# Sigmoid attention with a squared-ReLU MLP on one core: attn @ v in quarters of the array, and all eight PSUM banks as four tiles in turn

## The chip, the core and the metric

The kernel runs on one core of a Trainium2 chip. The core has a matrix engine (TensorE, in the profile PE, with its weight loads as PEld), a vector engine (DVE), a scalar engine (ACT), GpSimd (POOL), and a sync engine (SP) that issues the DMAs here. Each engine works through its own queue in order; semaphores make an engine wait for another. Matmul results land in PSUM, which this kernel uses as eight banks of 512 fp32 numbers on each of 128 partitions. The metric is the device time of one launch in microseconds. The kernel before takes 1073.21 us, the median of 3 runs (1072.75 to 1073.55).

## What is computed

```
def _attn_ref(q, k, v):                       # (8, 12, 448, 64) each
    scores = q @ k.T / sqrt(64) - log(448)
    return sigmoid(scores) @ v

def _moe_ref(x, w_in, w_out):                 # x: 3584 x 768, the heads side by side
    r = maximum(x @ w_in, 0)                  # 768 x 2048
    return (r * r) @ w_out                    # 2048 x 768
```

## The kernel before

There are two stages. The first is the attention, in 24 **blocks** of two **pairs**; a pair is two heads of one batch entry. `pairs` counts 48 pairs, and block d works on pairs n = 2d and n + 1. Beside the attention, this stage also converts the MLP's weights. The second stage is the MLP: `gemm1` and `gemm2`, each with seven products in place of eight on 2 x 2 blocks. The change only touches the first stage and the way in which PSUM is handed out.

For one pair, the transposed q and k of both heads lie in one tile `x` (head j on partitions 64j to 64j + 63). `high` (L489) and `low` (L493), both on DVE, split it into two parts of lower precision, `qh` and `ql`. The 448 keys are three tiles of 128 (NT = 3) and a rest of 64 (KR = 64).

- `scores` (L276): for each key tile, three passes (high with high, low with high, high with low) of two matmuls, one per head, each with 64 rows of weights by 128 columns. The form is written 64*128 in the profile, and the two run side by side in the array. The result, 128 keys by 2 heads x 448 queries, is a PSUM tile `sc` of two banks; ACT turns it into `at` by one sigmoid (L259).
- `scores_rest` (L292): the 64 left-over keys of both pairs in one PSUM tile `sr`, four matmuls in the form 64*64, one for each quarter of the array.
- `attn_v_rest` (L304): the left-over keys times v, four matmuls 64*64. They start the sums of both pairs, which are the two banks of one PSUM tile (`pav` in the profile).
- `attn_v` (L313): the three key tiles times v, two matmuls 128*64 side by side for each, added to the same sums.
- `put_x`: the sums go to SBUF as `xo`; ACT copies those of the first pair (L320), DVE those of the second (L322). From batch entry 2 on, SP stores them to HBM.

Each fp32 matmul of `scores_rest`, `attn_v_rest` and `attn_v` stands in the trace as two of equal shape.

The weights arrive as 64-bit words. `convert_words` (L147, L148, on ACT) and `convert_join` (L152, L153, L156 on DVE, then L159 on POOL) turn half a chunk into numbers, and `sums` (L168 to L171, DVE) forms four sums per chunk. A chunk is three pieces, numbered k; `weights_of` deals 40 pieces out over 43 places, one place for each pair.

The order on each engine is written by hand in `block(d)` under `manual_schedule`: what stands earlier in `block` is earlier in each queue. At the head of block d stand ACT's copy of pair n - 2, the weight piece of place n - 2, `high(n + 3)`, DVE's copy of pair n - 1, and `low(n + 3)`. Then come the scores of pairs n and n + 1, the left-over scores of the *next* block, `attn_v_rest`, another `high` and `low` around the weight piece of place n - 1, the ACT words, and `attn_v`.

In the attention, PSUM is three two-bank tiles `sc` in rotation and one two-bank tile `duo`. The two sums `pav` live in `duo`, and one of the six score tiles of each block (the first of the second pair; another one in the last block) also uses it.

Of the kernel before, what the change touches and what calls it, by code (L numbers as in the profile page):

```python
# [19 lines left out]
P = 128  # L20
# [50 lines left out]
def sigmoid_attention_relu2_mlp(  # L71
# [189 lines left out]

    def score_tile(name):
        return ps.tile([P, 2, 512], F32, tag="sc", bufs=3, name=name)[:, :, :S]

    def scores(b, p, x, passes=((0, 0), (1, 0), (0, 1))):

        out = []

        other = (0, 2) if (b, p) >= (B - 1, NP - 2) else (1, 0)
        for t in range(NT):  # L270
            sc = (duo if (p % 2, t) == other else score_tile)(f"sc_{b}_{p}_{t}")
            ks = slice(t * P, (t + 1) * P)
            for n, (kp, qp) in enumerate(passes):
                for j in range(2):
                    rows = slice(j * D, (j + 1) * D)
                    nc.tensor.matmul(  # L276
                        sc[:, j],
                        x[kp][rows, 1, ks],
                        x[qp][rows, 0],
                        start=(n == 0),  # L280
                        stop=(n == len(passes) - 1),
                    )
            out.append(sigmoid(f"at_{b}_{p}_{t}", sc))
        return out

    def scores_rest(d, xs):

        sc = score_tile(f"sr_{d}")
        for r, x in enumerate(xs):
# [6 lines left out]

    def attn_v_rest(d, rest, vt):

        sums = duo(f"pav_{d}")
        pavs = [sums[:, r] for r in range(2)]  # L300
        for r in range(2):
            for j in range(2):
                rows, columns = slice(r * KR, (r + 1) * KR), slice(j * D, (j + 1) * D)
                nc.tensor.matmul(  # L304
                    pavs[r][columns], vt[rows, 2 * NT, columns], rest[rows, j], start=True, stop=False
                )
        return pavs

    def attn_v(n, pav, at, vt):
        for t in range(NT):  # L310
            for j in range(2):
                columns = slice(j * D, (j + 1) * D)
                nc.tensor.matmul(  # L313
                    pav[columns], vt[:, n % 2 * NT + t, columns], at[t][:, j], start=False, stop=(t == NT - 1)
                )

    def put_x(b, p, pav, scalar=False):
        x = op1(f"xo_{b}_{p}")
        if scalar:
            nc.scalar.copy(out=x, in_=pav)  # L320
        else:
            nc.vector.tensor_copy(out=x, in_=pav)  # L322
        if b < KEPT:
# [75 lines left out]
    todo = [(m, i) for m in range(2) for i in range(NI) if m == 0 or i not in DEFERRED]  # L399
    x, vt, xs, at, pav, f64, w, rest = {}, {}, {}, {}, {}, {}, {}, {}  # L400
    ready, stores, later = [], [], []
# [30 lines left out]
    def block(d):  # L432

        n = 2 * d
        more = n + 2 <= last
        for m in (n + 5, n + 6):
            load(m)
# [5 lines left out]
        if d == 0:  # L445
            for m in (1, 2, 3):
                high(m)
                low(m)
            score(0, (x[0],), ((0, 0),))
            rest[0] = scores_rest(0, (x[0], x[1]))  # L450
# [46 lines left out]

    def put(n, scalar=False):
        stores.append(put_x(*pairs[n], pav.pop(n), scalar))

# [22 lines left out]

    def duo(name):
        return ps1.tile([P, 2, 512], F32, tag="duo", bufs=1, name=name)[:, :, :S]

    def bank(name):
        return ps2.tile([P, 512], F32, tag="bank", bufs=6, name=name)[:, :S]

# [216 lines left out]
    with tc.manual_schedule():  # L746
        with tc.tile_pool(name="ps", bufs=3, space=PSUM) as ps:
            wp = ps.tile([P, 2, 512], F32, tag="sc", bufs=3, name="warm_ps")[:, :, :S]
            for i in range(8):
# [6 lines left out]
            for k in range(2):  # L756
                weights_load(k)
            load(4)
            for d in range(len(pairs) // 2 - 2):
# [14 lines left out]
        ps2 = ctx.enter_context(tc.tile_pool(name="ps2", bufs=6, space=PSUM))  # L774
        work = [
# [64 lines left out]
```

## Time and profile before

| quantity | before |
|---|---|
| median of 3 runs | 1073.21 us |
| the profiled execution, its own time | 1072.65 us |
| its span, first to last instruction | 1070.9 us |
| attention, 4.2 to 249.8 us of the span: length | 245.6 us |
| busy in it: PE / DVE / ACT / POOL | 245.4 / 196.1 / 201.6 / 60.9 us |
| granted TensorE clock | 1.000 |

A row of the timeline has the start in us from the span's start, the length in us, the engine, the line of the kernel, the operation, output <- input with the shapes, a count where several are merged, and in brackets the idle time before it with what ended it. A row of groups has the same names, then busy time and the mean length of one in ns, then idle time before it. A matmul's length includes its way through the array, so neighbours overlap: the pace of the array is read from the distance between starts, not from lengths.

### The profile page before, as it was taken

The page shows a single profiled execution, that of the slowest core. Times are in us where ns is not written, and L with a number is a line of the kernel's source. Part 1 is how long each engine was busy: PE and PEld are TensorE (multiplying, and loading weights), DVE is VectorE, ACT ScalarE, POOL GpSimd, SP SyncE. Part 2 cuts the span into 40 slices and gives each one's busy share as a digit, 9 for nine tenths or more (in the row PEclk, how much of TensorE's full clock was granted, in tenths as well). Part 3 has the DMA queues.
Part 4 walks back from the last instruction along what each step waited for, and adds up shares of the span by engine and source line. Part 5 has one row for each costly group of instructions (what it writes and reads, how often), then busy time and mean ns, then how long its engine had stood idle before and what let it go on. Part 6 is the DMA issues. An engine that isn't in the chain of part 4 may idle for free.

```text
span 1070.9 us, 14914 instructions
## 1 busy us (share of the span) xinstructions
PE 1066.0 (100%) x5858; PEld 888.4 (83%) x5858; DVE 765.5 (71%) x865; ACT 621.1 (58%) x772; POOL 75.5 (7%) x42
## 2 busy tenths in 40 slices
PE   9999999999999999999999999999999999999998
PEld 4555555557999999999999999999999999999997
DVE  6887888776688898645579884456897925579941
ACT  7887888876767765433455653344565523455721
POOL 1222232210111000000000000000000000000000
PEclk9999999999999999999999999999999999999999
DMA  9989999882576445533343465333335633333441
GB/s 360 391 291 323 376 378 335 323 284 66 183 257 212 128 144 188 183 112 104 103 140 97 145 210 183 104 103 104 115 118 195 204 105 120 120 97 109 144 144 52
DMA packets 83446, 196.80 MB, mean 184 GB/s; under 512 B 6704, under 2 KB 57776, under 8 KB 83376
## 3 DMA queue, kind: packets, MB, share of 16 engines
q1 hardware_dynamic: 83376, 195.85, 53.1%
q8 instruction: 46, 0.75, 0.3%
q14 instruction: 24, 0.20, 0.0%
HBM read 154.53 MB, written 41.29 MB: 183 GB/s over the span
## 4 chain that ended last, share of the span: by engine, by line
PE 98%; DVE 1%; ACT 0%; issue 0%; ACTq 0%; DVEq 0%
PE ha L534 22%; PE oa L534 22%; PE hb L534 11%; PE ob L534 11%; PE pav L313 10%; PE sc L276 8%; PE hc L534 5%; PE oc L534 5%; PE sr L292 2%; PE pav L304 2%; PE warm_ps L750 0%; DVE xo L358 0%; ACT w_1h L236 0%; DVE xo L322 0%; ACT xt_0h L329 0%
## 5 line engine op out<-in xcount | busy, mean ns | idle before, releaser
L237 DVE TENSOR_TENSOR w_1l<-w_1l,w_1h 128x1536 fp32r<-128x1536 f32 x60 | 105.9, 1766 | 72.7 <-ACT w_1h L236 72.1
L577 ACT COPY s<-ha 128x448 f32<-128x448 f32 x96 | 51.0, 531 | 132.7 <-PE ha L534 122.9
L259 ACT ACTIVATE at<-sc 128x896 f32<-128x896 f32 x144 | 119.3, 934 | 10.5 <-PE sc L276 10.5
L313 PE MATMUL pav<-at,v 128*64 128x448 f32 x576 | 113.5, 543 | 0.0
L236 ACT CAST w_1h<-w_1l 128x1536 fp32r<-128x1536 f32 x60 | 88.8, 1480 | 19.6 <-DMA w_1l<-w 19.6
L313 PEld LDWEIGHTS pav<-at,v 128*64 128x64 f32 x576 | 39.2, 137 | 72.7 <-issue 72.2
L237 DVE TENSOR_TENSOR w_5l<-w_5l,w_5h 128x1152 fp32r<-128x1152 f32 x32 | 43.3, 1354 | 45.3 <-ACT w_5h L236 45.3
L159 POOL TENSOR_TENSOR a<-a,f 128x768 int32<-128x768 int32 x26 | 60.9, 2343 | 160.0 <-ACT at L259 64.4
L236 ACT CAST w_0h<-w_0l 128x1536 fp32r<-128x1536 f32 x28 | 41.5, 1480 | 47.8 <-DMA w_0l<-w 47.8
L237 DVE TENSOR_TENSOR w_0l<-w_0l,w_0h 128x1536 fp32r<-128x1536 f32 x28 | 49.2, 1756 | 18.9 <-ACT w_0h L236 18.6
L276 PE MATMUL sc<-qh 64*128 64x448 f32 x282 | 54.2, 381 | 0.2 <-DVE xo L322 0.2
L493 DVE TENSOR_TENSOR ql<-x,qh 128x896 fp32r<-128x896 f32 x47 | 54.1, 1151 | 0.1
L236 ACT CAST w_5h<-w_5l 128x1152 fp32r<-128x1152 f32 x32 | 37.1, 1158 | 25.5 <-DMA w_5l<-w 25.3
L276 PE MATMUL sc<-qh,ql 64*128 64x448 f32 x282 | 51.5, 362 | 0.0
L276 PE MATMUL sc<-ql,qh 64*128 64x448 f32 x282 | 51.4, 361 | 0.0
L614 DVE TENSOR_TENSOR g<-hb,s 128x448 f32<-128x448 f32 x32 | 19.9, 622 | 42.5 <-PE hb L534 42.5
L560 DVE SCALAR_TENSOR_TENSOR g<-g 128x896 f32<-128x896 f32 x40 | 43.6, 1090 | 1.1
L276 PEld LDWEIGHTS sc<-qh 64*128 64x128 f32 x282 | 26.4, 184 | 19.2 <-issue 12.7
L489 DVE CAST qh<-x 128x896 fp32r<-128x896 f32 x47 | 32.5, 691 | 8.6 <-DMA x<-qk 8.6
L702 ACT COPY t<-oa 128x448 f32<-128x448 f32 x36 | 19.1, 530 | 33.6 <-PE oa L534 33.2
L608 ACT ACTIVATE g<-ha 128x448 f32<-128x448 f32 x32 | 17.4, 544 | 31.7 <-PE ha L534 31.7
L534 PE MATMUL oa<-o_0h,w_0h 128*128 128x448 f32 x96 | 35.1, 365 | 0.0
(522 smaller groups left out, 3070.8 us busy)
## 6 DMA issues: line engine op xcount, KB each, us to landing
w_1l<-w SPq DMA_DIRECT2D x60, 768.0 KB, 4.5
w_0l<-w SPq DMA_DIRECT2D x28, 768.0 KB, 4.5
x<-qk SPq DMA_DIRECT2D x47, 448.0 KB, 7.0
f<-w_in SPq DMA_DIRECT2D x16, 768.0 KB, 8.0
w_5l<-w SPq DMA_DIRECT2D x32, 384.0 KB, 4.0
v<-v SPq DMA_DIRECT2D x24, 448.0 KB, 7.6
outT<-o SPq DMA_DIRECT2D x47, 224.0 KB, 2.4
w<-s SPq DMA_DIRECT2D x13, 768.0 KB, 9.6
```

Source lines behind the costliest of these rows:

```text
L159: nc.gpsimd.tensor_tensor(out=wb, in0=wb, in1=t.bitcast(I32)[:, :, 0], op=ALU.add)
L236: nc.scalar.copy(out=hi, in_=raw)
L237: nc.vector.tensor_sub(out=lo, in0=raw, in1=hi.bitcast(F32))
L259: nc.scalar.activation(at, sc, AF.Sigmoid, bias=NEG_LOG_S, scale=SCALE)
L276: nc.tensor.matmul(sc[:, j], x[kp][rows, 1, ks], x[qp][rows, 0], start=(n == 0), stop=(n == len(passes) - 1),)
L292: nc.tensor.matmul(sc[r * KR : (r + 1) * KR, j], x[rows, 1, NT * P :], x[rows, 0], start=True, stop=True)
L313: nc.tensor.matmul(pav[columns], vt[:, n % 2 * NT + t, columns], at[t][:, j], start=False, stop=(t == NT - 1))
L489: nc.vector.tensor_copy(out=xs[n][0], in_=x[n])
L493: nc.vector.tensor_sub(out=xs[n][1], in0=x[n], in1=xs[n][0].bitcast(F32))
L534: nc.tensor.matmul(out, a[:, c], b, start=first and n == 0, stop=last and n == 2, skip_group_check=True)
L560: nc.vector.scalar_tensor_tensor(out=t, in0=t, scalar=0.0, in1=t, op0=ALU.max, op1=ALU.mult)
L577: nc.scalar.copy(out=s, in_=banks["a", i])
```

## The change

`attn_v` now works in quarters. For each key tile, the keys 0 to 63 and 64 to 127 are separate matmuls (64*64), four per tile in place of two. The two halves are summed in two banks of one PSUM tile, so that each pair has a two-bank tile of its own. The left-over keys of the first pair go to its bank 0, those of the second pair to its bank 1, in `attn_v_rest`, which now stands between the `attn_v` of the two pairs.

To bring the two sums together, ACT copies bank 1 of each pair to `xo` (`take_x`), and DVE adds bank 0 to it (`put_x`). Both pairs need both operations.

`scores_rest` of a block moves from the middle of the block before to the head of its own, right behind `attn_v` of the pair before.

All eight banks are four two-bank tiles, handed out in turn by `two`: a block takes nine (`sr`, six `sc`, two `pav`), so that each takes the tile used four requests earlier. In the MLP the six banks of `bank` come from three pools in turn, as the same rotation over six.

`high` and `low` of a block now run one pair less ahead (`n + 2` at the head, `n + 3` behind), and so do the loads of x (`n + 4`, `n + 5`).

```diff
-    def attn_v_rest(d, rest, vt):
-        sums = duo(f"pav_{d}")
-        pavs = [sums[:, r] for r in range(2)]
+    def attn_v(n, sums, at, vt):
+        for t in range(NT):
+            for h in range(2):
+                rows = slice(h * KR, (h + 1) * KR)
+                for j in range(2):
+                    columns = slice(j * D, (j + 1) * D)
+                    nc.tensor.matmul(
+                        sums[columns, h],
+                        vt[rows, n % 2 * NT + t, columns],
+                        at[t][rows, j],
+                        start=(t == 0 and (n % 2, h) != (1, 1)),
+                        stop=(t == NT - 1 and (n % 2, h) != (0, 0)),
+                    )
+
+    def attn_v_rest(sums, rest, vt):
         for r in range(2):
             for j in range(2):
                 rows, columns = slice(r * KR, (r + 1) * KR), slice(j * D, (j + 1) * D)
                 nc.tensor.matmul(
-                    pavs[r][columns], vt[rows, 2 * NT, columns], rest[rows, j], start=True, stop=False
+                    sums[r][columns, r], vt[rows, 2 * NT, columns], rest[rows, j], start=(r == 1), stop=(r == 0)
                 )
...
-    def put_x(b, p, pav, scalar=False):
+    def take_x(b, p, sums):
         x = op1(f"xo_{b}_{p}")
-        if scalar:
-            nc.scalar.copy(out=x, in_=pav)
-        else:
-            nc.vector.tensor_copy(out=x, in_=pav)
+        nc.scalar.copy(out=x, in_=sums[:, 1])
+        return x
+
+    def put_x(b, p, sums, x):
+        nc.vector.tensor_add(out=x, in0=sums[:, 0], in1=x)
...
         else:
-            put(n - 2, True)
+            take(n - 1)
             weights_of(weights_join, n - 2)
-            high(n + 3)
+            put(n - 2)
+            high(n + 2)
             put(n - 1)
-            low(n + 3)
+            low(n + 2)
             for piece in later:
                 piece()
             later.clear()
             pieces_of(*T_PIECES.get(d, ()))
+            rest = scores_rest(d, (x[n], x[n + 1]))
             score(n, xs[n])
         score(n + 1, xs[n + 1])
-        if more:
-            rest[d + 1] = scores_rest(d + 1, (x[n + 2], x[n + 3]))
-        pav[n], pav[n + 1] = attn_v_rest(d, rest.pop(d), vt[d])
         for m in (n + 2, n + 3):
             weights_of(weights_load, m)
-        high(n + 4)
+        high(n + 3)
         weights_of(weights_join, n - 1)
-        low(n + 4)
-        for m in (n, n + 1):
-            weights_of(weights_words, m)
+        low(n + 3)
+        weights_of(weights_words, n)
...
+        for m in (n, n + 1):
+            pav[m] = two(f"pav_{m}")
         attn_v(n, pav[n], at[n], vt[d])
+        attn_v_rest((pav[n], pav[n + 1]), rest, vt[d])
+        take(n)
+        weights_of(weights_words, n + 1)
         attn_v(n + 1, pav[n + 1], at[n + 1], vt[d])
...
+    turn, pools = itertools.count(2), []
+
+    def two(name):
+        return duo(name, pools[next(turn) % 4])
...
             halve_weights(first[0, False])
             block(len(pairs) // 2 - 1)
             halve_weights(first[1, False])
+            take(last)
             put(last - 1)
-            put(last, True)
+            put(last)
```

What this does to the queues is shown at three places. Names end in running numbers; `sc_1_0_2` is key tile 2 of pair 0 of batch entry 1, and `pav_6` in the changed kernel is the sum of pair 6 (in the kernel before, `pav_2` is the sum tile of block 2).

**PE, from the end of one block's scores to the next block's.** Before (block 2):

```order
L276 MATMUL sc_0_5_2_364<-ql_5_205,qh_5_204 128x448 x2
L292 MATMUL sr_3_373<-x_1_0_96 64x448 x2
L292 MATMUL sr_3_373<-x_1_1_196 64x448 x2
L304 MATMUL pav_2_380<-rest_2_269,v_0_2_200 64x448 x4
L313 MATMUL pav_2_380<-at_0_4_0_326,v_0_2_200 64x448 x2
L313 MATMUL pav_2_380<-at_0_4_1_335,v_0_2_200 64x448 x2
L313 MATMUL pav_2_380<-at_0_4_2_344,v_0_2_200 64x448 x2
L313 MATMUL pav_2_380<-at_0_5_0_353,v_0_2_200 64x448 x2
L313 MATMUL pav_2_380<-at_0_5_1_362,v_0_2_200 64x448 x2
L313 MATMUL pav_2_380<-at_0_5_2_371,v_0_2_200 64x448 x2
L276 MATMUL sc_1_0_0_432<-qh_6_278 128x448 x2
```

In the changed kernel, one block later, on the same engine:

```order
L272 MATMUL sc_1_1_2_522<-ql_7_408,qh_7_407 128x448 x2
L303 MATMUL pav_6_544<-at_1_0_0_484,v_1_0_328 64x448 x4
L303 MATMUL pav_6_544<-at_1_0_1_493,v_1_0_328 64x448 x4
L303 MATMUL pav_6_544<-at_1_0_2_502,v_1_0_328 64x448 x4
L315 MATMUL pav_6_544<-rest_3_475,v_1_0_328 64x448 x2
L315 MATMUL pav_7_545<-rest_3_475,v_1_0_328 64x448 x2
L303 MATMUL pav_7_545<-at_1_1_0_511,v_1_0_328 64x448 x4
L303 MATMUL pav_7_545<-at_1_1_1_520,v_1_0_328 64x448 x4
L303 MATMUL pav_7_545<-at_1_1_2_529,v_1_0_328 64x448 x4
L288 MATMUL sr_4_597<-x_1_2_324 64x448 x2
L288 MATMUL sr_4_597<-x_1_3_326 64x448 x2
L272 MATMUL sc_1_2_0_604<-qh_8_465 128x448 x2
```

The array's form changed three times in a block before (64*128 to 64*64 to 128*64 and back); it now changes twice, since the left-over work and attn @ v share one form.

**DVE, where block 1 turns into block 2.** Before, a whole weight conversion (`a_0`), the split of pair 7, and the copy of pair 3's sum:

```order
L152 TENSOR_SCALAR a_0_179<-a_0_179 128x768
L153 TENSOR_SCALAR a_0_179<-a_0_179 128x768
L156 SCALAR_TENSOR_TENSOR a_0_179<-f64_0_0_1_90,a_0_179 128x768
L489 CAST qh_7_313<-x_1_1_196 128x896
L322 COPY xo_0_3_316<-pav_1_271 128x448
L493 TENSOR_TENSOR ql_7_314<-x_1_1_196,qh_7_313 128x896
```

Now, on the same engine at the same place:

```order
L153 TENSOR_SCALAR a_0_167<-a_0_167 128x768
L154 TENSOR_SCALAR a_0_167<-a_0_167 128x768
L157 SCALAR_TENSOR_TENSOR a_0_167<-f64_0_0_1_96,a_0_167 128x768
L325 TENSOR_TENSOR xo_0_2_307<-pav_2_289,xo_0_2_307 128x448
L494 CAST qh_6_337<-x_1_0_204 128x896
L325 TENSOR_TENSOR xo_0_3_330<-pav_3_290,xo_0_3_330 128x448
L498 TENSOR_TENSOR ql_6_338<-x_1_0_204,qh_6_337 128x896
```

The add of pair 2 stands between the conversion and the cast, and the add of pair 3 behind the cast. In PSUM's turn, the tile of pair 2's sum goes to the next block's second score tile, and that of pair 3's to its third; PE's first matmul of each waits for DVE.

**DVE and ACT, where the last block begins.** DVE before:

```order
L358 TENSOR_TENSOR xo_1_5_765<-xo_1_5_765,xo_1_2_643 128x448
L237 TENSOR_TENSOR w1_0_0_1l_2567<-w1_0_0_1l_2567,w1_0_0_1h_2566 128x1536
L322 COPY xo_7_3_2687<-pav_22_2648 128x448
L333 TENSOR_TENSOR xt2_0l_2668<-xo_1_3_652,xt2_0h_2667 128x448
```

DVE now:

```order
L498 TENSOR_TENSOR ql_47_2974<-x_7_5_2766,qh_47_2973 128x896
L238 TENSOR_TENSOR w1_0_0_1l_2892<-w1_0_0_1l_2892,w1_0_0_1h_2891 128x1536
L325 TENSOR_TENSOR xo_7_2_2997<-pav_44_2979,xo_7_2_2997 128x448
L325 TENSOR_TENSOR xo_7_3_3029<-pav_45_2980,xo_7_3_3029 128x448
L336 TENSOR_TENSOR xt2_0l_3012<-xo_1_3_711,xt2_0h_3011 128x448
```

ACT now:

```order
L321 COPY xo_7_2_2997<-pav_44_2979 128x448
L332 CAST xt2_0h_3011<-xo_1_3_711 128x448
L332 CAST xt2_0h_3011<-xo_1_4_817 128x448
L332 CAST yt2_0_3013<-xo_1_5_839 128x448
L237 CAST w1_0_0_1h_2891<-w1_0_0_1l_2892 128x1536
L321 COPY xo_7_3_3029<-pav_45_2980 128x448
L260 ACTIVATE rest_23_3044<-sr_23_3039 128x896
```

The split of the MLP's first weights (a cast on ACT, then a subtraction on DVE) stands ahead of both adds of the block before, where it stood ahead of one copy; ACT's copy of pair 44 stands ahead of the casts, where it stood behind them.

More of the change, by code (lines that the diff above doesn't have):

```diff
@@ L1 @@
+import itertools
 import math
@@ L496, in score, with take, put @@
         at[n] = scores(*pairs[n], *args)
-    def put(n, scalar=False):
-        stores.append(put_x(*pairs[n], pav.pop(n), scalar))
+    def take(n):
+        xo[n] = take_x(*pairs[n], pav[n])
+    def put(n):
+        stores.append(put_x(*pairs[n], pav.pop(n), xo.pop(n)))
     def weights_of(piece, n):
@@ L746, in sigmoid_attention_relu2_mlp @@
     with tc.manual_schedule():
-        with tc.tile_pool(name="ps", bufs=3, space=PSUM) as ps:
-            wp = ps.tile([P, 2, 512], F32, tag="sc", bufs=3, name="warm_ps")[:, :, :S]
+        with ExitStack() as attention:
+            pools += [attention.enter_context(tc.tile_pool(name=f"two{i}", bufs=1, space=PSUM)) for i in range(3)]
+            pools.append(ps1)
+            wp = two("warm_ps")
             for i in range(8):
```

33 lines of the change are left out of this document (11 added, 22 removed).

## The prediction

> **What bounds the kernel now.** I read the page first, then the chain of waits, then the timeline of each engine around two blocks. From the page, the busy times and the chain that ended last:
>
> ```profile
> PE 1066.0 (100%) x5858; PEld 888.4 (83%) x5858; DVE 765.5 (71%) x865; ACT 621.1 (58%) x772; POOL 75.5 (7%) x42
> PE 98%; DVE 1%; ACT 0%; issue 0%; ACTq 0%; DVEq 0%
> ```
>
> PE never rests, so the time can only fall by what PE itself saves, and any wait that PE gets is paid in full. PE's timeline, windows about one attention block, from the start of block 14's `attn_v` to that of block 15's:
>
> ```profile
> 154.01 4.73 PE L313 MATMUL pav<-at,v 128*64 128x448 f32 x24
> ...
> 158.19 0.55 PE L313 MATMUL pav<-at,v 128*64 128x448 f32 x2
> 158.67 0.47 PE L276 MATMUL sc<-qh 64*128 64x448 f32 x2
> 158.98 0.37 PE L276 MATMUL sc<-qh,ql 64*128 64x448 f32 x2
> ...
> 162.22 0.36 PE L276 MATMUL sc<-ql,qh 64*128 64x448 f32 x2
> 162.51 0.61 PE L292 MATMUL sr<-x 64*64 64x448 f32 x4
> ...
> 162.94 0.56 PE L292 MATMUL sr<-x 64*64 64x448 f32 x4
> 163.31 0.56 PE L304 MATMUL pav<-rest,v 64*64 64x448 f32 x4
> ...
> 163.69 0.56 PE L304 MATMUL pav<-rest,v 64*64 64x448 f32 x4
> 164.17 0.60 PE L313 MATMUL pav<-at,v 128*64 128x448 f32 x2
> ```
>
> A block is 164.17 - 154.01 = 10.16 us. Call a **slot** what starts together. Four quarters have the next four behind them after 0.37 or 0.38 us (162.94, 163.31, 163.69). Two halves keep the same pace: the twelve slots of `attn_v` from 154.01 to the last at 158.19 are eleven steps, 0.38 each. So a quarter slot does the work of a half slot in the same time, and cutting `attn_v` in quarters gains nothing by itself.
>
> **The gain: one change of form less.** Into 128*64, the step 163.69 to 164.17 is 0.48 in place of 0.375, and the first slot behind a change is 0.05 longer (162.51 to 162.94: 0.43). That change goes: 0.16 us a block. The other two stay: into the scores, 158.19 to 158.67 (0.48) and 158.67 to 158.98 (0.31 in place of 0.20); out of them, 162.22 to 162.51 (0.29). That the step from `sr` to the scores costs no more is seen in block 0, the only place where they follow each other now:
>
> ```profile
> 7.05 0.98 PE L292 MATMUL sr<-x 64*64 64x448 f32 x8
> 7.97 0.47 PE L276 MATMUL sc<-qh 64*128 64x448 f32 x2
> 8.28 0.39 PE L276 MATMUL sc<-qh,ql 64*128 64x448 f32 x2
> ```
>
> 7.05 + 0.43 = 7.48, then 0.49 and 0.31: as behind `attn_v`. Term one: 24 x 0.16 = **-3.8 us**, a block of 10.01.
>
> The number of matmul rows in `attn_v` doubles. The Trainium skill, TensorEngine Tiling (Array Packing), Instruction Overhead, charges every matmul some 60 cycles and warns against splitting what is small already; at 2.4 GHz (TensorE: Matmul & The Clock Gate, first table) 576 more rows of 25 ns would be an estimated 14.4 us. The quarter slots at 163.31 and 163.69 hold twice the matmuls of a half slot at the same pace, so here they show none of it.
>
> **The price: PE now waits for the sums to be fetched.** Set a block's zero at its first `sr` slot. The scores start at 0.43 + 0.49 = 0.92, the second score tile at 0.92 + 0.31 + 2 x 0.20 = 1.63, the third at 2.23. In the turn of four tiles the second takes the sum tile of the block's before last pair, the third that of its last pair. Before, those tiles had other banks; the scores waited for no fetch, but in the last block. Now each waits for ACT's copy and DVE's add. But DVE works in order, and between the two adds stands the cast of `high`. The rows of POOL, DVE and ACT about the head of block 2:
>
> ```profile
> 21.40 2.57 POOL L159 TENSOR_TENSOR a<-a,f 128x768 int32<-128x768 int32 x1 [20.96 <-ACT at L259]
> 26.12 2.13 POOL L159 TENSOR_TENSOR a<-a,f 128x768 int32<-128x768 int32 x1 [2.14 <-DVE a L156]
> ...
> 21.18 1.08 DVE L493 TENSOR_TENSOR ql<-x,qh 128x896 fp32r<-128x896 f32 x1
> 22.18 2.21 DVE L152 TENSOR_SCALAR a<-a 128x768 f32<-128x768 f32 x1
> 24.43 0.56 DVE L153 TENSOR_SCALAR a<-a 128x768 int32<-128x768 int32 x1
> 25.03 0.96 DVE L156 SCALAR_TENSOR_TENSOR a<-f,a 128x768 int32<-128x768 int32 x1
> 25.90 0.62 DVE L489 CAST qh<-x 128x896 fp32r<-128x896 f32 x1
> 27.18 0.62 DVE L322 COPY xo<-pav 128x448 f32<-128x448 f32 x1 [0.66 <-ACT xo L320]
> ...
> 26.62 0.53 ACT L320 COPY xo<-pav 128x448 f32<-128x448 f32 x1 [1.95 <-PE pav L313]
> ```
>
> The last `attn_v` slot starts 0.375 ahead of zero and ends at 0.17; with ACT's copy (0.53) and an add as long as DVE's copy (0.62), the second add can end by 1.4 at best, and 2.23 leaves 0.8 of slack.
>
> POOL's join starts 1.09 behind the start of L156. While it runs, DVE's work from SBUF stands: L152 at 22.18 ends at 24.39, 0.42 behind POOL's end (23.97), and takes 2.21, where the two operations after it take 0.56 and 0.96. The cast at 25.90 slipped in 0.22 ahead of POOL. With an add in front of it, it no longer does. How long it is then held, block 14 shows (POOL's end 156.78, the cast's 157.26: 0.48 behind):
>
> ```profile
> 154.18 2.60 POOL L159 TENSOR_TENSOR a<-a,f 128x768 int32<-128x768 int32 x1 [3.68 <-ACT at L259]
> 154.97 2.29 DVE L489 CAST qh<-x 128x896 fp32r<-128x896 f32 x1
> ```
>
> The MLP has the very order, conversion, add from PSUM and SBUF, then work from SBUF alone:
>
> ```profile
> 273.46 0.56 DVE L156 SCALAR_TENSOR_TENSOR b<-fd,b 128x384 int32<-128x384 int32 x1
> 273.94 0.62 DVE L614 TENSOR_TENSOR g<-hb,s 128x448 f32<-128x448 f32 x1
> 274.47 2.32 DVE L237 TENSOR_TENSOR w_1l<-w_1l,w_1h 128x1536 fp32r<-128x1536 f32 x1
> 274.15 1.02 POOL L159 TENSOR_TENSOR b<-b,fd 128x384 int32<-128x384 int32 x1 [52.76 <-DVE b L156]
> ```
>
> The add takes 0.62 beside POOL, no more than the copy at 27.18, and what follows is 0.56 longer than its like at 239.30 (1.76, last rows below).
>
> That the loser waits for the whole instruction is the rule of the Trainium skill, SBUF — State Buffer, Who interferes with whom; were the port shared by halves instead, the cast would take 1.24 and the price below would be near nothing. The 2.29 us of the cast speak for the rule.
>
> Block 2 walked through, from block 1's zero: the first add may start at once, the cast behind it at 0.66, the second add 1.12, `ql` 1.66, cast 2.66, conversion 3.20 with L156 at 4.39, `ql` 5.26, POOL from 5.48 to 8.05; L152 of the next conversion is held to 8.47, L156 at 9.11, add 9.98, POOL from 10.20 to 12.33, the cast held to 12.81, second add to 13.35. Block 2's zero is 10.01, so PE has the tile at 3.40 (0.06 for the signal) and wanted it at 2.23: 1.17, and 0.11 for the longer first slot, **1.28 us**. With the old DVE times as they stand, add done at 29.27 against a tile due at 26.50 - 0.92 - 0.16 + 2.23 = 27.65, it is 1.8; with DVE 0.5 earlier than I walk it, 0.8.
>
> How often: eight of POOL's joins begin within 0.7 us before a block's first scores, that of block 2 at 26.12 (scores at 26.50) and the last, in block 21:
>
> ```profile
> 219.25 2.14 POOL L159 TENSOR_TENSOR a<-a,f 128x768 int32<-128x768 int32 x1 [2.14 <-issue]
> ...
> 34.93 2.10 POOL L159 TENSOR_TENSOR a<-a,f 128x768 int32<-128x768 int32 x1 [6.67 <-DMA v<-v]
> ```
>
> They belong to blocks 2, 5, 10, 13, 14, 16, 18 and 21. Four more, the first at 34.93, begin 1.5 us or more ahead (scores at 36.67); there the second add ends at 2.0 to 2.3, at the edge, 0 to 0.2 each. Term two: 8 x 1.3 = **+10.4** (6.4 to 15).
>
> Two more places. In block 14, ACT has three casts of the MLP's operands behind its words; they push the copy of the last sum to 1.41 to 1.94, the add to 2.60: **+0.5** in block 15. And the last block, where the MLP's first weights are split ahead of both adds:
>
> ```profile
> 236.35 1.08 ACT L329 CAST xt_0h<-xo 128x448 fp32r<-128x448 f32 x2
> 237.27 0.62 ACT L329 CAST yt<-xo 128x448 fp32r<-128x448 f32 x1
> 237.74 1.53 ACT L236 CAST w_1h<-w_1l 128x1536 fp32r<-128x1536 f32 x1
> 239.30 1.76 DVE L237 TENSOR_TENSOR w_1l<-w_1l,w_1h 128x1536 fp32r<-128x1536 f32 x1 [3.95 <-ACT w_1h L236]
> 240.97 0.62 DVE L322 COPY xo<-pav 128x448 f32<-128x448 f32 x1
> 241.12 0.37 PE L276 MATMUL sc<-ql,qh 64*128 64x448 f32 x2
> 241.65 0.47 PE L276 MATMUL sc<-qh 64*128 64x448 f32 x2 [0.16 <-DVE xo L322]
> ```
>
> ACT's copy of pair 44 at 7.97 now precedes the casts, so these end at 9.79 and the weight cast at 11.32, 1.31 in the last block; DVE subtracts to 3.02, the first add ends at 3.64, and the second score tile wanted it at 1.63: 2.2 with signal and restart. The 0.44 that PE loses there now (scores at 241.12, next due 241.32, came at 241.65, and 0.11) goes. **+1.7**.
>
> The rest is hidden, in the attention's idle time (columns: stretch, length, then busy us of PE, PEld, DVE, ACT and POOL):
>
> ```profile
> 4.20:249.80 245.60, 245.44 (x1819) 130.10 (x1818) 196.08 (x270) 201.60 (x257) 60.92 (x26) 1.00 0.89 331
> ```
>
> 24 more ACT copies (0.53) are 12.7 us in 44.0 that ACT idles, 24 more DVE operations (0.62) 14.9 in 49.5; without that cover they would cost their whole length. The loads run a pair less ahead, but so do their users. SP's stores wait for the second add, and the next block's loads queue behind them, at most 2 us later; x is needed over a block later. The MLP keeps its rotation of banks.
>
> **Sum**: -3.8 + 10.4 + 0.5 + 1.7 = **+8.8 us** on the profiled execution's 1072.65, whose span is 1070.9 and which lies 0.56 below the median of the runs: 1081.5 there, 1082.0 as a median.
>
> **Rivals.** (1) The third score tile isn't late: DVE is far enough ahead that the cast is through, and the second add done by 2.23, or the cast isn't held. Then -3.8 remains, with or without 2.2 of the two smaller waits: 1069.4 to 1071.6. For it: the cast at 25.90 did slip in. Against: the add that now stands in front takes 0.54, POOL comes after 0.22. The point of decision is the second add's end at 2.23; 17 in 100, half of them by over 0.2% (a difference this measurement can tell from none). (2) Quarters hold 0.43 a slot over a long run, as their first step does: 24 x 12 x 0.055 = 15.8 more, about 1093 with the waits partly covered; against it stand 163.31 and 163.69; 6 in 100. (It is what the rule on the overhead of each matmul would look like.) (3) The form changes cost the same in total, as the next change takes over what the old one cost: 3.8 more than forecast, 1086; block 0 speaks against it; 4 in 100. My forecast has 73.
>
> **The numbers.** The terms' bounds give -3.8 + 6.4 + 0 + 1 = +3.6 up to -3.8 + 15 + 1.3 + 1.7 = +14.2, so 1077 to 1087. The case (1) lies below; to leave out no more than 2 in 10, the range is 1075 to 1088. Faster 0.09; the same 0.11, with (1)'s other half and the smallest waits; slower 0.80.
>
> **What would show it.** In the changed profile: PE idle at the second and third score tiles, released by DVE's add, about a microsecond each in the eight blocks named and two in the last; casts of 2 us or more behind an add; blocks elsewhere of 10.0 us. Wrong, if those casts keep their 0.62, if PE waits nowhere, or if undisturbed blocks aren't 0.16 shorter.

## The result, and the profile after

The changed kernel takes 1081.43 us, the median of 16 executions (1080.62 to 1086.6); the kernel before, measured beside it, 1073.32 us (16 executions). The ratio is 1.0068, 95% interval 1.0048 to 1.0087: slower, by 8.1 us from median to median.

| quantity | before | after |
|---|---|---|
| profiled execution, its own time | 1072.65 us | 1085.26 us |
| its span | 1070.9 us | 1083.2 us |
| MLP's first product starts at | 249.85 us | 258.28 us |

The profiled execution lies 3.8 above its median, because TensorE's pace fell by 2% at about 858 us of its span, in the MLP, which the change doesn't touch (last section); the attention, up to 258 us, isn't affected. From the page, busy times, the chain that ended last, and one group, under it the same group before; then TensorE's waits (line, releaser, us in total, times, longest); then the attention's stretch, with the columns of the prediction's:

```profile
PE 1069.8 (99%) x6434; PEld 892.7 (82%) x6434; DVE 788.0 (73%) x889; ACT 634.0 (59%) x796; POOL 72.5 (7%) x42
PE 87%; DVE 7%; ACT 2%; issue 1%; DMA 1%; POOL 0%; SPq 0%; ACTq 0%; DVEq 0%
L494 DVE CAST qh<-x 128x896 fp32r<-128x896 f32 x47 | 46.1, 982 | 7.0 <-DMA x<-qk 7.0
```
```profile
L489 DVE CAST qh<-x 128x896 fp32r<-128x896 f32 x47 | 32.5, 691 | 8.6 <-DMA x<-qk 8.6
```
```profile
PE sc L272 <- DVE xo L325: 8.6, 10, 2.0
```
```profile
4.20:260.00 255.80, 247.10 (x2403) 136.18 (x2403) 218.20 (x294) 214.19 (x282) 57.99 (x26) 1.00 0.86 318
```

DVE's share of the chain that ended last was 1% and is 7% now. TensorE's waits for DVE come to 8.6 us in ten places, all at score tiles that wait for DVE's add. In the stretch PE's idle time has gone from 0.2 to 8.7 us, and the mean cast of `high` has grown from 691 ns (32.5 us for 47, before) to 982.

**An undisturbed block** (PE, the end of block 2 and the start of block 3):

```profile
31.79 2.49 PE L303 MATMUL pav<-at,v 64*64 64x448 f32 x24
34.10 0.93 PE L315 MATMUL pav<-rest,v 64*64 64x448 f32 x8
34.85 2.44 PE L303 MATMUL pav<-at,v 64*64 64x448 f32 x24
37.10 0.93 PE L288 MATMUL sr<-x 64*64 64x448 f32 x8
37.97 0.47 PE L272 MATMUL sc<-qh 64*128 64x448 f32 x2
38.28 0.36 PE L272 MATMUL sc<-qh,ql 64*128 64x448 f32 x2
```

From 31.79 to 37.10 are fourteen quarter slots (56 rows, four to a slot): 0.43 for the first, behind the change of form, and (5.31 - 0.43) / 13 = 0.375 for the others. There is no step of 0.48 any more. From `sr` to the scores it is 37.97 - 37.10 = 0.87, which is 0.375 and 0.49. The distance between the starts of `sr` is 10.01 us in the blocks without a wait, where it was 10.16 or 10.17.

**A block with a wait**, block 2, on PE, DVE and POOL:

```profile
28.31 0.37 PE L272 MATMUL sc<-ql,qh 64*128 64x448 f32 x2
29.15 0.47 PE L272 MATMUL sc<-qh 64*128 64x448 f32 x2 [0.48 <-DVE xo L325]
...
25.12 0.96 DVE L157 SCALAR_TENSOR_TENSOR a<-f,a 128x768 int32<-128x768 int32 x1
26.00 0.62 DVE L325 TENSOR_TENSOR xo<-pav,xo 128x448 f32<-128x448 f32 x1
26.53 2.03 DVE L494 CAST qh<-x 128x896 fp32r<-128x896 f32 x1
28.48 0.61 DVE L325 TENSOR_TENSOR xo<-pav,xo 128x448 f32<-128x448 f32 x1
...
26.21 1.87 POOL L160 TENSOR_TENSOR a<-a,f 128x768 int32<-128x768 int32 x1 [2.14 <-DVE a L157]
```

POOL begins at 26.21, beside the first add; the cast then stands until POOL is through at 28.08 and ends 0.48 later; the second add ends at 29.09, and PE, due at 28.31 + 0.20 = 28.51, starts at 29.15. It loses 0.64 and then 0.11 by the longer first slot, 0.75 in all: the block is 10.76 long.

**The last block**, on ACT, DVE and PE:

```profile
243.85 0.53 ACT L321 COPY xo<-pav 128x448 f32<-128x448 f32 x1 [1.20 <-PE pav L315]
244.28 1.03 ACT L332 CAST xt_0h<-xo 128x448 fp32r<-128x448 f32 x2
245.21 0.56 ACT L332 CAST yt<-xo 128x448 fp32r<-128x448 f32 x1
245.68 1.47 ACT L237 CAST w_1h<-w_1l 128x1536 fp32r<-128x1536 f32 x1
...
247.18 1.76 DVE L238 TENSOR_TENSOR w_1l<-w_1l,w_1h 128x1536 fp32r<-128x1536 f32 x1 [3.99 <-ACT w_1h L237]
248.86 1.15 DVE L325 TENSOR_TENSOR xo<-pav,xo 128x448 f32<-128x448 f32 x2
...
249.62 0.47 PE L272 MATMUL sc<-qh 64*128 64x448 f32 x2 [2.00 <-DVE xo L325]
```

Both adds stand behind the subtraction of the weights, which waited for three casts and the weights' cast on ACT.

### The profile page after: what moved, and what is told of

Read it like the earlier page. It is cut to its first block, busy times and chain, and to the rows that moved or that the text cites. A ratio compares the mean times of both kernels' runs of the same rounds, so it can differ in the third digit from the quotient of the medians.

```text
span 1083.2 us, 16127 instructions
## 1 busy us (share of the span) xinstructions
PE 1069.8 (99%) x6434; PEld 892.7 (82%) x6434; DVE 788.0 (73%) x889; ACT 634.0 (59%) x796; POOL 72.5 (7%) x42
## 4 chain that ended last, share of the span: by engine, by line
PE 87%; DVE 7%; ACT 2%; issue 1%; DMA 1%; POOL 0%; SPq 0%; ACTq 0%; DVEq 0%
PE ha L547 22%; PE oa L547 22%; PE hb L547 11%; PE ob L547 11%; PE pav L303 5%; PE oc L547 5%; PE hc L547 5%; PE sc L272 5%; DVE qh L494 2%; DVE ql L498 1%; DVE xo L325 1%; DVE a L153 1%; PE pav L315 1%; ACT at L260 1%; PE sr L288 1%
## 5 line engine op out<-in xcount | busy, mean ns | idle before, releaser
L303 PE MATMUL pav<-at,v 64*64 64x448 f32 x1152 | 118.1, 540 | 0.0
L303 PEld LDWEIGHTS pav<-at,v 64*64 64x64 f32 x1152 | 41.6, 133 | 60.8 <-issue 52.8
L160 POOL TENSOR_TENSOR a<-a,f 128x768 int32<-128x768 int32 x26 | 58.0, 2230 | 168.4 <-DVE a L157 80.3
L494 DVE CAST qh<-x 128x896 fp32r<-128x896 f32 x47 | 46.1, 982 | 7.0 <-DMA x<-qk 7.0
L498 DVE TENSOR_TENSOR ql<-x,qh 128x896 fp32r<-128x896 f32 x47 | 50.9, 1082 | 0.1
L321 ACT COPY xo<-pav 128x448 f32<-128x448 f32 x48 | 26.2, 547 | 28.7 <-PE pav L303 14.2
L325 DVE TENSOR_TENSOR xo<-pav,xo 128x448 f32<-128x448 f32 x48 | 29.5, 617 | 12.0 <-ACT xo L321 11.8
```

The source lines that it names most:

```text
L160: nc.gpsimd.tensor_tensor(out=wb, in0=wb, in1=t.bitcast(I32)[:, :, 0], op=ALU.add)
L303: nc.tensor.matmul(sums[columns, h], vt[rows, n % 2 * NT + t, columns], at[t][rows, j], start=(t == 0 and (n % 2, h) != (1, 1)), stop=(t = ...
L325: nc.vector.tensor_add(out=x, in0=sums[:, 0], in1=x)
L494: nc.vector.tensor_copy(out=xs[n][0], in_=x[n])
L498: nc.vector.tensor_sub(out=xs[n][1], in0=x[n], in1=xs[n][0].bitcast(F32))
```

## The experiments

Times are medians; "before" is the kernel before on the same chip. The ratio and its interval are those on record; they differ from the quotient of the two medians by up to 0.0014 (e2: 1.0002, where the medians give 1.0016). All but e6 build on the changed kernel.

| label | what it is | us | ratio to before, 95% interval |
|---|---|---|---|
| e1_adds_first | both adds ahead of the cast | 1075.08 | 1.0031 (1.0007 to 1.0054) |
| e2_no_pool | no add on POOL | 1074.89 | 1.0002 (0.9975 to 1.0029) |
| e6_before_no_pool | the kernel before, no add on POOL | 1073.01 | 0.9995 (0.9975 to 1.0015) |
| e3_last | the last block alone mended | 1078.47 | 1.0050 (1.0036 to 1.0063) |
| e4_all | e1, e3, and ACT's three casts later | 1070.98 | 0.9981 (0.9972 to 0.9990) |
| e7_adds_ahead | e4, and the adds ahead of the conversion too | 1071.56 | 0.9995 (0.9971 to 1.0018) |
| e9_sums_behind | e7, DVE's four sums a block later | 1077.78 | 1.0041 (1.0028 to 1.0054) |
| e10_splits_later | e7, two splits of MLP operands a block later | 1070.38 | 0.9974 (0.9964 to 0.9985) |
| e5_halves | e7 with halves, left-over keys first | 1088.91 | 1.0147 (1.0133 to 1.0162) |
| e8_rest_behind | e7 with halves, left-over keys behind | 1086.87 | 1.0130 (1.0113 to 1.0147) |
| e11_rest_behind | e8 once more | 1073.07 | 0.9999 (0.9990 to 1.0008) |

Block lengths in us, from one start of `sr` to the next in the profiled executions; blocks that aren't listed take 10.00 to 10.10, but for the first. The last one, 23, is counted to the MLP's first product.

| block | after | e1 | e2 | e4 | e7 | e10 |
|---|---|---|---|---|---|---|
| 2 | 10.76 | 10.00 | 10.01 | 10.01 | 10.01 | 10.01 |
| 5 | 10.85 | 10.01 | 10.01 | 10.01 | 10.01 | 10.01 |
| 7 | 10.00 | 10.14 | 10.00 | 10.16 | 10.01 | 10.01 |
| 10 | 10.96 | 10.01 | 10.00 | 10.00 | 10.01 | 10.01 |
| 13 | 11.16 | 10.66 | 10.59 | 10.03 | 10.01 | 10.01 |
| 14 | 11.30 | 10.25 | 10.01 | 10.86 | 11.02 | 10.01 |
| 15 | 10.61 | 10.61 | 10.63 | 10.01 | 10.01 | 11.07 |
| 16 | 11.22 | 10.01 | 10.01 | 10.01 | 10.00 | 10.02 |
| 17 | 10.03 | 11.05 | 10.01 | 10.48 | 10.01 | 10.01 |
| 18 | 11.35 | 10.02 | 10.00 | 10.04 | 10.01 | 10.00 |
| 20 | 10.01 | 10.38 | 10.01 | 10.40 | 10.01 | 10.01 |
| 21 | 11.00 | 10.03 | 10.00 | 10.01 | 10.01 | 10.00 |
| 22 | 10.01 | 10.01 | 10.01 | 10.08 | 10.98 | 10.01 |
| 23 | 12.39 | 12.44 | 13.94 | 10.12 | 10.12 | 10.12 |

### Both adds ahead of the cast

```diff
             put(n - 2)
-            high(n + 2)
             put(n - 1)
+            high(n + 2)
             low(n + 2)
```

> The changed kernel with both adds of a block's head ahead of the cast of high; the work of each engine is the same. Held-cast theory: the second add no longer waits for GpSimd, the nine waits of the third score tile at a block's head (8.6 us with the restarts) go but for block 15's (0.6, ACT's copy is late there), and the time falls from 1081.4 to about 1073. Load theory (the vector engine has too much to do with 24 more operations): the same work in another order, 1081 to 1082.

1075.08 us: 6.3 less than the changed kernel, and 2 more than expected. In block 2 (DVE and POOL) the two adds now run one behind the other, beside POOL, and the cast meets only what is left of POOL's operation:

```profile
26.48 1.15 DVE L325 TENSOR_TENSOR xo<-pav,xo 128x448 f32<-128x448 f32 x2
27.54 1.50 DVE L494 CAST qh<-x 128x896 fp32r<-128x896 f32 x1
...
26.69 1.87 POOL L160 TENSOR_TENSOR a<-a,f 128x768 int32<-128x768 int32 x1 [2.14 <-DVE a L157]
```

Six of the eight long blocks are gone and 13 and 14 have shrunk; 17 and 20 are new ones. So the place of the cast between the adds is what cost most, and not the number of operations: DVE and ACT do as many as before this edit. What is left has another cause, which e4 and e7 look for.

### POOL's add left out

```diff
-        nc.gpsimd.tensor_tensor(out=wb, in0=wb, in1=t.bitcast(I32)[:, :, 0], op=ALU.add)
```

In e2_no_pool and e6_before_no_pool the converted weights lack their low part.

> The changed kernel without GpSimd's add of the weight conversion, so the converted weights lack their low part; order and work of the other engines stay. Held-cast theory: every cast takes 0.62, the second add ends before the third score tile is due, about 1073; only the last block's wait (2.2) and block 15's (0.6) stay. Load theory: 1080 or more, since the vector engine's work is the same.

Block 2 on DVE, in the order of the changed kernel, add, cast, add:

```profile
24.93 0.62 DVE L324 TENSOR_TENSOR xo<-pav,xo 128x448 f32<-128x448 f32 x1 [0.44 <-ACT xo L320]
25.47 0.62 DVE L493 CAST qh<-x 128x896 fp32r<-128x896 f32 x1
27.21 0.62 DVE L324 TENSOR_TENSOR xo<-pav,xo 128x448 f32<-128x448 f32 x1 [1.13 <-ACT xo L320]
```

The cast takes 0.62, and DVE even waits for ACT ahead of the second add. All eight long blocks are as short as any other, but 13 (10.59). Block 15, which the prediction puts down to ACT's three casts, stays at 10.63, as it should. Block 13 has the same cause, which the prediction didn't count there: ACT runs three casts from 136.55 to 138.04, its copy follows at 137.94, and DVE's second add waits for it:

```profile
138.50 0.62 DVE L324 TENSOR_TENSOR xo<-pav,xo 128x448 f32<-128x448 f32 x1 [2.29 <-ACT xo L320]
```

In the changed kernel the held cast, which ends later, hides this. Of the 8.5 us that the eight blocks lose there, 8.0 go with POOL's add. The mechanism is shown from both sides: without POOL the order does no harm, and with the other order POOL does little.

The time, 1074.89, is 1.9 above what was expected. Of this, 0.6 is block 13, and about 1.5 a fall of the granted clock in the last block (last section).

> The kernel before without GpSimd's add in the conversion of weights (the low part of the converted weights is left out of the result). It asks whether the kernel before too pays for the casts that GpSimd's add holds up. Theory (no wait of TensorE there ends on VectorE or ScalarE in blocks 1 to 22): 1072.8 to 1073.6 us, the same as before. Rival (leaving the add out gains by itself, and the gain of e2_no_pool is partly that): 1068 us or less.

1073.01 against 1073.11 us: the kernel before gains nothing when POOL's add goes. In the attention of this run, TensorE's only wait for DVE or ACT is 0.2 us in all, for DVE's copy in the last block, as in the kernel before.

### The last block, and ACT's casts

```diff
         score(n + 1, xs[n + 1])
+        behind()
...
-            halve_weights(first[0, False])
-            block(len(pairs) // 2 - 1)
+            block(len(pairs) // 2 - 1, lambda: halve_weights(first[0, False]))
```

> The changed kernel with the split of the MLP's first weights moved from the last block's head to behind its scores. If the last block's 2.0 us of wait is what the forecast says, 1079.2; if what follows it would have waited anyway, 1081.4.

1078.47 us, 3.0 below the changed kernel and 0.7 below what was expected; the 0.7 isn't accounted for. The wait in the last block is gone, and from its `sr` to the MLP's first product it takes 254.68 - 244.56 = 10.12 us in place of 258.28 - 245.89 = 12.39. The nine other long blocks stay, each within 0.1 us of the changed kernel's.

e4_all takes this, the order of e1, and, for block 15, ACT's casts of the MLP's operands:

```diff
         score(n + 1, xs[n + 1])
+        for name in PIECES.get(d, ()):
+            pieces[name](later)
...
         attn_v(n + 1, pav[n + 1], at[n + 1], vt[d])
-        for name in PIECES.get(d, ()):
-            pieces[name](later)
```

> Both moves, and ACT's casts of the MLP's operands moved to behind the block's scores. If the three kinds of wait are all that the change costs, only the form changes' 3.8 us remain: every block 10.0 us, 1069.5 to 1070. If there is a further cost of the quarters or of the tiles in turn, 1073 or more.

1070.98 us, 2.2 below the kernel before, and 1 more than was expected. Block 15 is down to 10.01; with e1 and e3 alone it stayed at 10.61, so ACT's casts were its cause. Block 13, which e1 left at 10.66, is down to 10.03 by the same edit. Blocks 7, 14, 17 and 20 are still long.

### What stands ahead of the adds

Ahead of both adds there is still the weight conversion. e7_adds_ahead moves it behind them:

```diff
             take(n - 1)
-            weights_of(weights_join, n - 2)
             put(n - 2)
             put(n - 1)
+            weights_of(weights_join, n - 2)
```

> The changed kernel with both adds of the pair before ahead of the conversion of weights and of the casts on VectorE, ScalarE's copies ahead of its three casts, and the last block's scores ahead of the split of the MLP's weights. Theory (what is left of the waits comes from the conversion, which stands ahead of the adds and is late itself): every block takes 10.01 us, no wait of TensorE on VectorE's add is left but that of block 0, and the time is 1069.0 to 1069.8 us, 4 below the kernel before (24 changes of form at 0.16). Rival (the adds, which VectorE must now wait for, hold the conversion and the casts up, and these come late for the block after next): long blocks at other places, and 1071 us or more.

1071.56 us, where e4 had 1070.98. Blocks 17 and 20 are mended, 14 and 22 are 1.0 too long. The theory fell; long blocks at other places and a time of 1071 or more are what the rival said. DVE up to the wait of block 14, and PE:

```profile
136.25 0.62 DVE L325 TENSOR_TENSOR xo<-pav,xo 128x448 f32<-128x448 f32 x1 [0.90 <-ACT xo L321]
...
139.50 2.63 DVE L499 TENSOR_TENSOR ql<-x,qh 128x896 fp32r<-128x896 f32 x1
142.06 1.15 DVE L336 TENSOR_TENSOR x_0l<-xo,x_0h 128x448 fp32r<-128x448 f32 x2
...
144.20 0.54 DVE L169 TENSOR_TENSOR s<-a 128x384 f32<-128x384 f32 x1
...
147.20 1.15 DVE L325 TENSOR_TENSOR xo<-pav,xo 128x448 f32<-128x448 f32 x2
...
147.87 0.47 PE L272 MATMUL sc<-qh 64*128 64x448 f32 x2 [0.69 <-DVE xo L325]
```

At the head of block 13 DVE waits 0.90 us for ACT's copy, ahead of the second add; the conversion now stands behind that, as the rival had it. From there to 148.35 DVE doesn't rest. It has a subtraction that takes 1.55 us longer beside POOL (2.63 against 1.08), the MLP's splits (1.7) and the four sums (2.0) at once. e9_sums_behind moves the sums behind the adds of the next block:

```diff
             put(n - 1)
+            weights_of(weights_sums, n - 3)
+            for store in ready:
+                store()
+            ready.clear()
             weights_of(weights_join, n - 2)
+            weights_of(weights_sums, n - 2)
...
         weights_of(weights_join, n - 1)
+        if not more:
+            weights_of(weights_sums, n - 1)
```

> As e7_adds_ahead, but the four sums of converted weights that VectorE computes behind its second conversion of a pair of blocks (L169 to L172, 2 us) come one block later, behind the adds. Theory (what was left of the waits in e7_adds_ahead, 1.0 us each in blocks 14 and 22, is VectorE's queue ahead of the adds: these sums and the splits of the MLP's operands): no block but the first longer than 10.1 us, 1068.8 to 1070.0 us, 1.5 to 2 less than e7_adds_ahead and 0.3 to 0.4% below the kernel before. Rival (the two waits come from the splits and the held subtraction alone, or move a block on): two long blocks remain and the time is that of e7_adds_ahead within 0.7 us.

1077.78 us, with waits in six other blocks (4, 7, 12, 15, 17 and 20, each about 11.4 us long): the theory fell, and so did the rival, which had two. In block 3 and up to the wait in block 4, on DVE and then PE, one sees why:

```profile
36.42 0.55 DVE L169 TENSOR_TENSOR s<-a 128x384 f32<-128x384 f32 x1
...
39.61 0.96 DVE L157 SCALAR_TENSOR_TENSOR a<-f,a 128x768 int32<-128x768 int32 x1
40.48 0.62 DVE L505 CAST qh<-x 128x896 fp32r<-128x896 f32 x1
41.14 2.63 DVE L509 TENSOR_TENSOR ql<-x,qh 128x896 fp32r<-128x896 f32 x1
...
47.28 1.15 DVE L325 TENSOR_TENSOR xo<-pav,xo 128x448 f32<-128x448 f32 x2
...
47.95 0.47 PE L272 MATMUL sc<-qh 64*128 64x448 f32 x2 [1.15 <-DVE xo L325]
```

The sums fell into blocks that have a conversion in each half, and DVE was behind by the end of them. From 35.88 to 48.43 it doesn't rest.

e10_splits_later leaves the sums and moves the splits to where no sums are:

```diff
-PIECES = {12: (1,), 14: (2,), 20: (3,), 22: (6,)}
+PIECES = {13: (1,), 14: (2,), 21: (3,), 22: (6,)}
```

> As e7_adds_ahead, but two of the splits of the MLP's operands (pieces 1 and 3: two casts on ScalarE each, and three subtractions that VectorE does a block later) come one block later, where VectorE has no four sums in the same block. Theory (VectorE's queue ahead of the adds of block 14 is too long by 1 us, sums 2.0 and splits 1.7 together; either alone has room): no wait is left at the score tiles of blocks 1 to 22, the spans shrink by 2 us against e7_adds_ahead, 1069 to 1070 us. Rival (as in e9_sums_behind, what is moved makes another block late): two or more long blocks, 1071 us or more.

1070.38 us, 2.8 below the kernel before and the fastest measured here. One wait is left, in block 15:

```profile
PE sc L272 <- DVE xo L325: 0.8, 1, 0.8
```

Theory and rival both missed: the theory had no wait and 1069 to 1070 us, the rival two or more long blocks and 1071 or more. Of e7's two long blocks one is gone and one has moved, from 14 to 15.

### Quarters against halves

e5_halves computes attn @ v in halves again, with one sum for each pair and the left-over keys first (`x` is then ACT's copy alone):

```diff
-        attn_v(n, pav[n], at[n], vt[d])
         attn_v_rest((pav[n], pav[n + 1]), rest, vt[d])
+        attn_v(n, pav[n], at[n], vt[d])
...
-            for h in range(2):
-                rows = slice(h * KR, (h + 1) * KR)
-                for j in range(2):
...
+            for j in range(2):
+                columns = slice(j * D, (j + 1) * D)
+                nc.tensor.matmul(
+                    sums[columns, 0], vt[:, n % 2 * NT + t, columns], at[t][:, j], start=False, stop=(t == NT - 1)
+                )
...
-        nc.vector.tensor_add(out=x, in0=sums[:, 0], in1=x)
```

> As e7_adds_ahead, but attn @ v in halves of the array (128 rows by 64 columns) with one sum for each pair, as the kernel before computes it, with the scores of the left-over keys behind it: the array changes its form four times in a block instead of twice, and there is no add of a second sum. Theory (a change of form costs 0.1 to 0.3 us, and quarters run at the pace of halves): 24 blocks longer by about 0.3 us than those of e7_adds_ahead, 1075 to 1077 us. Rival (the gain of e7_adds_ahead over the kernel before comes from elsewhere, and a change of form costs nothing): the same time as e7_adds_ahead within 1 us.

1088.91 us, 12 more than the theory had; the rival, no more than e7, is further off. Blocks take 10.81 to 10.91. PE, its weight loads, and ACT in block 14 (rows of a short window each):

```profile
151.38 0.59 PE L309 MATMUL pav<-rest,v 64*64 64x448 f32 x2
...
151.81 1.04 PE L309 MATMUL pav<-rest,v 64*64 64x448 f32 x6
...
152.31 0.54 PE L309 MATMUL pav<-rest,v 64*64 64x448 f32 x2
152.78 0.60 PE L301 MATMUL pav<-at,v 128*64 128x448 f32 x2
...
151.88 0.19 PEld L309 LDWEIGHTS pav<-rest,v 64*64 64x64 f32 x4 [0.30 <-ACT at L260]
...
150.88 1.76 ACT L260 ACTIVATE at<-sc 128x896 f32<-128x896 f32 x2
```

The left-over keys' product takes three slots, of two, four and two rows, where the kernel before needs two of four. The second pair's half of it waits: by the turn of four, its tile is the one that the fourth score tile of the block had, and ACT's fourth sigmoid, the first of the two from 150.88, ends at about 151.83. That is the extra 0.5 us a block; about 0.35 are left for the two more changes of form. The run didn't single the changes out, so e8_rest_behind puts the left-over keys behind both pairs, in front of `sr`, which has their form:

```diff
-        attn_v_rest((pav[n], pav[n + 1]), rest, vt[d])
         attn_v(n, pav[n], at[n], vt[d])
-        take(n)
         weights_of(weights_words, n + 1)
         attn_v(n + 1, pav[n + 1], at[n + 1], vt[d])
+        attn_v_rest((pav[n], pav[n + 1]), rest, vt[d])
+        take(n)
```

> As e5_halves (attn @ v in halves, one sum for each pair, no second add), but attn @ v of the left-over keys behind both pairs and so in front of the scores of left-over keys, which have the same form: the array changes its form three times in a block, as in the kernel before. Theory (the gain of the quarters is one change of form, 0.155 us a block; the 0.5 us more of e5_halves is a wait of the left-over keys' product for the bank of the fourth score tile): blocks of 10.16 us, 1072.5 to 1074 us. Rival (a change of form costs nothing, and the blocks of 10.01 come from the four tiles or the moved scores): blocks of 10.01, 1069 to 1070 us.

The blocks are 10.16 and 10.17 long, as forecast, and the MLP's first product starts at 249.66. But the time was 1086.87 us: in the MLP, PE's pace had fallen by 2%, and that part took 835.5 us in place of 821.0. The same code again:

> e8_rest_behind once more, the same code. There the attention took what was expected (blocks of 10.16 and 10.17 us, MLP's first product at 249.66 us, 0.19 before the kernel before), but TensorE's pace in the MLP fell by 2% at about 350 us of the span, with a granted clock of 1.00, and the MLP took 835.5 us in place of 821.0. Theory (the slower pace comes and goes by execution, as in the profiled execution of the changed kernel from 858 us on, and has nothing to do with the order of the attention): some executions at 1072.5 to 1074. Rival (the order of this kernel brings the slower pace on): all executions at 1085 or more again.

1073.07 us, 1073.21 for the kernel before, and blocks of 10.16 and 10.17 again. So with four tiles in turn, the moved scores and all the mending of e7, halves cost what they cost before; the 0.155 us a block belong to the quarters. Slots have the same pace in both (0.375), so what is left as the cause is one change of form less.

Why e8's MLP was slow stays open. All four executions of e8, on one chip, were at 1085 or more, and all eleven of e11, on another, were not. The chip alone isn't it: e9_sums_behind, measured on e8's chip beside it, had its MLP at 821.1 us.

## Why the prediction was right

It said 1082.0 us and slower; measured were 1081.43. Step by step, from the profiled executions:

| step | forecast | measured |
|---|---|---|
| 24 blocks, one change of form less | -3.8 | -3.7 |
| held cast, eight blocks | +10.4 | +8.5 |
| joins at the edge | 0 to 0.2 each | +0.2 in all |
| block 15 | +0.5 | +0.6 |
| last block | +1.7 | +1.8 |
| sum | +8.8 | +7.4 |
| MLP's first product, later by | | +8.4 |

- **The gain.** 10.01 in place of 10.165 us a block, at 0.375 a slot. Rival (2), slots of 0.43, fell with the fourteen slots above, and rival (3), changes that cost the same in total, with e10 and e11: 10.01 with two changes, 10.165 with three.
- **The held cast.** The eight blocks named are the eight long ones. They lose 0.75 to 1.34 us, 1.07 in the mean, where 1.3 was forecast: the step was right and its size a fifth too high. In block 13, 0.58 of the 1.15 would have been lost without the held cast too, to ACT's casts (e2, e4); the prediction counted these for block 15 alone. In block 2, walked in the prediction, POOL took 1.87, where it began beside an add that reads PSUM, in place of the 2.13 read from before, where it began beside the cast; and DVE's L157 stood 0.3 earlier (1.22 ahead of the block's zero at 26.34, against 0.90). Rival (1), a third tile that isn't late, was true for the other blocks alone. e2 shows that POOL is the cause and e1 that the order is.
- **The rule of the whole instruction.** The prediction weighed a rule of the Trainium skill, SBUF — State Buffer, Who interferes with whom, by which the loser waits for the other's whole operation. The trace agrees: the cast ends 0.48 behind POOL's end in block 2. By an evenly shared port it would have taken an estimated 1.24 (twice 0.62) from 26.53, and the add behind it would have ended at about 28.3, ahead of PE's 28.51: it would have cost nothing.
- **Block 15 and the last block.** 10.61 - 10.01 = 0.6, gone in e4. In the last block 12.39 - 10.12 = 2.27, less the 0.44 that before lost there: 1.8. Both causes were undone one by one (e4, e3).
- **What the sum lacked.** The terms come to 7.4 and the MLP starts 8.4 later. Of the difference, 0.6 lies ahead of block 0, whose `sr` starts at 7.66 against 7.05; in the other profiled executions with `sr` at the head of its block it starts anywhere from 6.79 to 8.13, so this isn't put down to the change. The other 0.4 isn't accounted for; the first block, which waits for loads, varies by as much (8.24 to 8.83 us, 8.67 in the changed kernel). And the changed kernel spends 2.0 us outside its span (1.85 to 2.07) where the kernel before spends 1.8: 0.2 that was in no term. It doesn't come with the quarters as such: e2 and e9 have them and spend 1.8 (1.73 to 1.85), e1, e4, e7 and e10 spend 2.1; its cause stays open. The error of the big term, 1.9 too high, was partly made up by these. So that the median came within 0.6 us of the forecast is in part luck; the places, the causes and the order of the sizes are not.
- **The slope.** The 3.7 us that the quarters gain can be had: e10 has 2.8 of them.

## What to carry to other kernels

Where banks are handed out in turn, fetching a sum becomes part of the next product's way, and what counts is then not how busy the fetching engine is (DVE 73%) but what stands in its queue ahead of the fetch when the tile is due. Look in the trace for the operations of that queue that another engine can hold up, and put the fetch ahead of them; an operation that takes 0.62 us alone can cost a bottleneck engine more than a microsecond. Moving work off such a place pays only if the place it goes to has room: of the two moves made from e7, e10's gained 1.2 us and e9's lost 6.2.

## What the hardware showed that I had not expected

**Behind a wait of 2 us the clock can fall to half.** In e2_no_pool PE waits 2.00 us in the last block, to 241.53. The windows behind that (columns as above; the clock is third from the end):

```profile
241.00:244.00 3.00, 2.47 (x18) 2.50 (x20) 3.00 (x7) 1.68 (x3) 0.00 (x0) 0.78 0.00 0
244.00:246.00 2.00, 2.00 (x14) 1.94 (x12) 1.13 (x3) 1.62 (x3) 0.00 (x0) 0.50 0.00 0
246.00:251.00 5.00, 5.00 (x56) 2.00 (x56) 0.00 (x0) 2.71 (x4) 0.00 (x0) 0.99 0.02 3
```

From 242.7 to 246.1 the granted clock is 0.50, the scores go on at 0.37 a slot in place of 0.20, and the last block takes 13.94 us in place of 12.4: 1.5 more than the wait itself. The changed kernel's profiled execution has the same wait and a clock of 1.00 behind it. Of its 16 executions, five have a mean granted clock of 0.998, and these are the times from 1082.13 up, but for the profiled 1085.26; in e2 all ten have 0.997 to 0.999, and in e3_last, without that wait, all four have 1.000. This makes the link likely and doesn't prove it: four executions are few, where the fall lies in the executions without a trace wasn't seen, and a mean of 0.999 can come from elsewhere (e4's profiled execution, without the wait, has it from a clock of 0.50 in the span's last 1.1 us). The Trainium skill, TensorE: Matmul & The Clock Gate, Part 1, has the clock at half rate after an idle window of about 3.4 us; here a wait of 2.0 was followed by it, in some executions and not in others.

**TensorE can go 2% slower at a granted clock of 1.00.** The same stretch of the MLP in e8_rest_behind and in e11_rest_behind, which are the same code:

```profile
500.00:600.00 100.00, 100.00 (x486) 90.83 (x485) 73.04 (x72) 50.36 (x60) 0.00 (x0) 1.00 0.37 118
```
```profile
500.00:600.00 100.00, 100.00 (x496) 92.68 (x495) 77.30 (x75) 54.38 (x64) 0.00 (x0) 1.00 0.37 118
```

PE is busy all the time in both; 486 matmuls in 100 us against 496. In e8 the slower pace began at about 350 us of the span. In the changed kernel's profiled execution it began at 858:

```profile
700.00:800.00 100.00, 100.00 (x495) 92.69 (x494) 72.90 (x72) 48.96 (x59) 0.00 (x0) 1.00 0.34 110
900.00:1000.00 100.00, 100.00 (x486) 90.83 (x485) 68.81 (x67) 47.37 (x57) 0.00 (x0) 1.00 0.34 109
```

Single executions of other kernels lie 10 to 14 us above their median (1083.33 of the kernel before, 1085.27 of e7), where 2% of the MLP's 821 us would make 16; whether they have this cause wasn't seen, nor what brings it on.
